# A mixture-of-experts kernel behind strided attention: hints for table jumps in the common part, 32 levels, an earlier load and clears on another engine

## The chip, the core and the metric

The kernel runs on one core of one Trainium2 chip. The time is device microseconds of one execution. A core has TensorE (PE, with its weight loads shown apart as PEld), VectorE (DVE), ScalarE (ACT), GpSimd (POOL) and SyncE (SP, which here issues most transfers), and 16 DMA engines. Each engine has a sequencer of its own that reads its own instructions; a branch is taken by every engine for itself.

## The reference

Two stages in float32. First attention for 8 batches of 8 heads, 576 positions, 64 wide: heads 0 to 3 look back at most 31 positions (local), heads 4 to 7 at every 32nd position (strided). Then each of the 4608 rows (512 wide) goes to the one of eight experts with the highest gate logit; the expert is a two-layer perceptron with 1024 hidden units, and its result is scaled by the gate's probability.

```python
mask_local = (rel >= 0) & (rel < 32)
mask_strided = (rel >= 0) & (pos[None, :] % 32 == pos[:, None] % 32)
...
attn = np.exp(scores - np.max(scores, axis=-1, keepdims=True))
...
for e in range(E):
    h = np.maximum(x_sorted[lo:hi] @ w1[e], 0.0)
    y_sorted[lo:hi] = h @ w2[e]
...
return gate_w[:, None] * y
```

## The kernel before

**Attention.** The program goes through the batches in steps. For a batch SP loads the strided queries and keys (`load_s`: qs and ks, four transfers), the strided values (`load_vs`: vs, four), the local queries and keys (`load_l`: ql and kl, in pieces) and the local values (`load_vl`: vl, four). PE transposes qs and ks (L204) and ql and kl (L192), multiplies queries with keys (L227, L232 and others), and multiplies the weights with vl (L347). Of vl every block of 32 positions is needed twice, for itself and as the block before; POOL makes the second copy (`load_prev`, L123). A few buffers (VL[1], VS[1], BD[0], BD[1]) have parts that must be zero and are never loaded; they are cleared once, by memsets. SP's transfers go in the order in which the program writes them.

**Routing.** The gate's logits give every row its expert and its place in that expert's list. The rows are counted per expert, and the count becomes a level: the number of entries of the table TOTALS that lie under the count (row `lev`, seven DVE instructions from `cnf` to `lvi`). An expert's rows are then rounded up to that entry. By count of this case's data the eight experts have 591, 497, 610, 490, 661, 437, 657 and 665 rows.

**Experts.** For each expert the program has a common part (`first(e)`), which works on the first 256 rows and is the same for any count, and a tail (`rest(e, n)`), which is written out once for every entry n of the table. Between them each engine loads the level (`level`, a TENSOR_LOAD, L869) and takes a jump through a table to the tail of that level (shown as COMPARE_BRANCH, L1196); a tail ends with an unconditional branch to the next common part. `tc.switch_hint` emits, on each engine, an instruction that names the coming jump's target ahead of time (BRANCH_PREFETCH_HINT). In `hid(f, ...)` PE makes one eighth of the hidden layer (L638 to L640: three products, since the float32 numbers are split in a high and a low part), in `mm2c` and `mm2r` the second layer (L916 to L918, L656 to L658). `zs` is a piece of the second layer of the expert before that is left over for the common part and the start of the next tail: `zs((2,))` is step 2 of eight, three matmuls (L656 to L658 of z). `spread` puts pieces of other work between such steps.

Before, a hint for expert 1 stands at the head of `first(1)`, and the hints for experts 2 to 7 in the tail of the expert before, eight steps ahead of its end. The hint for expert 0 and those for the exit of a tail are not part of the change. In the trace COMPARE_BRANCH at L1196 is the jump into a tail as well as the exit out of it.

Of the kernel before, what the change touches and what calls it, by code (L numbers as in the profile page):

```python
# [32 lines left out]
C0 = 256  # L33
N0 = C0 // TM
PB = B - 2
STEPS = range(400, 688, 8)
TOTALS = (C0, 384, *STEPS, 720, CAP)


@with_exitstack  # L40
def kernel(ctx, tc, q, k, v, w_gate, w1, w2, out):
# [42 lines left out]
    def load_s(b):  # L84

        for nm, src, dst in (("qs", q, qs), ("ks", k, ks)):
            t = dst[b] = ld.tile([128, 18 * D], F32, name=nm)
            nc.sync.dma_start(t[:, :16 * D], bass.AP(tensor=src.tensor, offset=base(src, b, 4), ap=[[16 * D, 128], [1, 16 * D]]))
            nc.sync.dma_start(t[:, 16 * D:], bass.AP(tensor=src.tensor, offset=base(src, b, 4) + 64 * 32 * D,
                                                     ap=[[2 * D, 128], [1, 2 * D]]))  # L90

    def load_vs(b):
        for rq in range(4):
            nc.sync.dma_start(VS[b % 2][32 * rq:32 * rq + NB],
                              bass.AP(tensor=v.tensor, offset=base(v, b, 4) + rq * 512,
                                      ap=[[32 * D, NB], [S * D, 4], [1, 512]]))

    def load_l(b, jjs=range(5)):
        for jj in jjs:
            for nm, src, dst in (("ql", q, ql), ("kl", k, kl)):  # L100
                if jj == 0:
                    dst[b] = ld.tile([128, 5, 4, D], F32, name=nm)
                n = 128 if jj < 4 else 64
                nc.sync.dma_start(dst[b][:n, jj], bass.AP(tensor=src.tensor, offset=base(src, b, 0) + jj * 128 * D,
                                                          ap=[[D, n], [S * D, 4], [1, D]]))
# [69 lines left out]
    for i in range(2):  # L175
        V.memset(PST[i][:, :, NB:], 0.0)
    V.memset(VS[0], 0.0)

    wg = const.tile([128, 4, 32], F32)
    V.memset(wg, 0.0)  # L180
# [208 lines left out]
    def lg_a(b):  # L389
        xl, xs = XL.pop(b), XS.pop(b)  # L390
        ls = LS[b] = wk.tile([128, 2, S // 2], F32, name="ls")
        for hf in range(2):
# [15 lines left out]
    colr = const.tile([RT, TM], F32, name="colr")  # L408
    G.iota(colr, pattern=[[1, TM]], base=0, channel_multiplier=0, allow_small_or_imprecise_dtypes=True)
    lev = const.tile([1, len(TOTALS) - 1], F32, name="lev")  # L410
    G.iota(lev[:, 2:2 + len(STEPS)], pattern=[[STEPS.step, len(STEPS)]], base=STEPS.start, channel_multiplier=0,
           allow_small_or_imprecise_dtypes=True)
    for i, n in enumerate(TOTALS[:-1]):
        if n not in STEPS:
# [188 lines left out]
    def gather(e, t, rows=NTOK + 1):  # L603
        G.indirect_dma_start(out=XG[t], out_offset=None, in_=x_out[:rows, :],  # L604
                             in_offset=bass.IndirectOffsetOnAxis(ap=src[:, NT * e + t:NT * e + t + 1], axis=0))
# [91 lines left out]
            return f((n - d) // 5)  # L697

    load_l(0, (2, 3, 4))
    load_vs(0)  # L700
    load_vl(0)
    for n in range(-1, N + 3):
# [8 lines left out]
            open_w()  # L711
        if bb < B:
            if m == 0 and n >= 0:
                if n == 0:
                    load_s(1)
                load_l(bb, (0, 1))
                if n == 0:
                    load_prev(0)
            if m == 1:
                load_l(bb, (2, 3, 4))  # L720
            if m == 2:
                load_vs(bb)
            if m == 3:
                load_vl(bb)
                if bb + 1 < B and n > 0:
                    load_s(bb + 1)
            if m == 4 and n > 0:
                load_prev(bb)
        if n == 0:
            V.memset(VL[1][:, :, 0:1], 0.0)  # L730
            V.memset(BD[0], 0.0)
            blank_s(1)
        if n == 1:
            V.memset(VS[1], 0.0)
            V.memset(BD[1], 0.0)
            blank_l(1)
        if n == 1:
            nc.sync.dma_start(wg[:, :, :8], bass.AP(tensor=w_gate.tensor, offset=w_gate.offset,
# [75 lines left out]
    def settle(n):  # L814
        for _ in range(min(n, len(evs))):
            evs.pop(0)()
# [27 lines left out]
    take(4)  # L844
    rank_c(b)
    slots(slice(N0, NC))
    V.tensor_copy(cnf, cnt)
    V.tensor_tensor(lvc, cnf[:, :, None].to_broadcast([1, E, nl - 1]), lev[:, None, :].to_broadcast([1, E, nl - 1]),
                    op=OP.is_gt)
# [2 lines left out]
    V.tensor_reduce(lvf[:, 2 * E:], lvf[:, E:2 * E], axis=AX.X, op=OP.add)  # L852
    V.tensor_scalar(lvf[:, E:2 * E], lvf[:, E:2 * E], 0.0, float(NTOK), op0=OP.is_gt, op1=OP.mult)
    V.tensor_copy(lvi, lvf)
    for t in range(N0, NT):
        gather(0, t)
    settle(9)
    take(99)
    split2(0, 0)
    settle(9)  # L860
    for i in range(1, 4):
# [124 lines left out]

    def first(e):

        if e == 1:
            tc.switch_hint(lv[e], nl, label=f"e{e}")  # L990
        if e == 0:
            V.memset(YT, 0.0)
            for t in range(NT):
                gather(1, t)
                if t > 2 and t % 2:
                    scatter(0, t // 2 - 1)
        elif e + 1 < E:
            turn()
        if e:
            unturn()  # L1000
        if e == 0:
            for f in refill(0)[1::2]:
                f()
            turn()
        elif e == 1:
            spread(refill(e), [lambda f=f: hid(f, 0, C0) for f in range(6)])
        else:
            zs(range(2, 6))
        if e + 1 < E:
            level(e + 1)  # L1010

    def rest(e, n):
# [7 lines left out]
        nd = direct(w) if last and not one else 0  # L1020
        cy = slice(TM if one else C0 + TM * nd, C0 + w)
        if e > 1:
            zs((6, 7))
            done(e - 1, 0, Z)
            scatter(e - 1, 0)

# [62 lines left out]
        if cy.stop > cy.start:  # L1089
            cols = [mm2c(cy, d) for d in range(4)]  # L1090
            steps += [lambda g=g: next(g) for g in cols for f in range(8)]
        if e and not last:
            steps.insert(max(len(steps) - 8, 0), lambda: tc.switch_hint(lv[e + 1], nl, label=f"e{e + 1}"))
        k = len(todo)
        for i, f in enumerate(steps):
            f()
# [104 lines left out]
```

## Time and profile before

| | |
|---|---|
| time, median of 3 runs | 672.06 us (669.59 to 676.34) |
| time of the profiled execution | 675.38 us |
| span of the profiled execution | 673.5 us |
| mean granted TensorE clock | 0.957 of full speed |
| PE busy | 613.1 us, 91% |
| DVE, ACT, POOL busy | 376.9, 321.6, 202.9 us |

The span goes from the first to the last instruction; the 1.9 us between it and the time lie around it. Busy time is summed per engine, so engines overlap. The granted clock says which share of full speed the throttle gave PE. Attention takes about the first 240 us, the experts the rest.

### The profile page before, as it was taken

The numbers are of one execution on the slowest core, as the hardware profiler recorded it, in microseconds if no ns is written. First come the engines' busy times: TensorE is split into PE (matmuls) and PEld (weight loads), VectorE is DVE, ScalarE is ACT, GpSimd is POOL, SyncE is SP. The second block draws the span as 40 slices with busy tenths as digits, with TensorE's granted clock in tenths as the row PEclk, the third lists the DMA queues.
The fourth block names the chain that finished last, engine by engine and source line by source line (L and its number), as shares of the span: only waits on it lengthen the run. The fifth ranks groups of instructions, "written<-read, shape, count | busy, mean of one in ns | idle before, by whom it ended". The sixth has DMA issues, their size and how long they took to land.

```text
span 673.5 us, 18414 instructions
## 1 busy us (share of the span) xinstructions
PE 613.1 (91%) x7270; PEld 539.7 (80%) x7270; DVE 376.9 (56%) x807; ACT 321.6 (48%) x647; POOL 202.9 (30%) x348
## 2 busy tenths in 40 slices
PE   5589899889996979979999999989999989999995
PEld 4467676667674869979999988879999879999994
DVE  6666888768798663664645346434436534445200
ACT  6457767747765332443543533532534633434311
POOL 0222256236255663503304304303303210110212
PEclk9689999879898889979999999989999989999999
DMA  9897788778635457668899579877368986344101
GB/s 199 172 228 180 188 219 200 178 179 206 162 112 191 153 199 175 165 162 153 294 167 180 212 160 178 295 134 179 141 165 160 260 217 100 148 141 79 51 33 57
DMA packets 237930, 114.02 MB, mean 169 GB/s; under 512 B 209053, under 2 KB 211101, under 8 KB 237728
## 3 DMA queue, kind: packets, MB, share of 16 engines
q1 hardware_dynamic: 230096, 89.70, 55.7%
q0 software_dynamic: 7632, 22.03, 10.9%
q8 instruction: 77, 1.26, 0.8%
q14 instruction: 125, 1.02, 0.5%
HBM read 74.47 MB, written 21.83 MB: 143 GB/s over the span
## 4 chain that ended last, share of the span: by engine, by line
PE 64%; issue 13%; SPq 9%; DVE 4%; ACT 4%; DMA 3%; POOL 2%; POOLq 0%; DVEq 0%; ACTq 0%
PE h L639 7%; PE h L638 7%; PE h L640 7%; SPq L944 5%; PE y L916 4%; PE y L917 4%; PE y L918 4%; PE o L347 2%; PE t L204 2%; PE t L192 2%; PE y L656 2%; PE y L657 2%; PE y L658 2%; SPq L612 2%; PE sc L232 2%
## 5 line engine op out<-in xcount | busy, mean ns | idle before, releaser
L639 PE MATMUL h<-x,w1h 128*128 128x256 f32 (+6 forms) x416 | 133.6, 321 | 3.7 <-issue 3.7
L638 PE MATMUL h<-xh,w1h 128*128 128x256 f32 (+6 forms) x416 | 133.6, 321 | 0.0
L640 PE MATMUL h<-xh,w1l 128*128 128x256 f32 (+6 forms) x416 | 133.3, 320 | 0.0
L645 DVE SCALAR_TENSOR_TENSOR hl<-h,hh 128x256 fp32r<-128x256 f32 (+6 forms) x104 | 52.4, 508 | 125.1 <-ACT hh L644 107.8
L644 ACT ACTIVATE hh<-h 128x256 fp32r<-128x256 f32 (+6 forms) x104 | 46.7, 454 | 117.1 <-PE h L640 104.3
L639 PEld LDWEIGHTS h<-x,w1h 128*128 128x128 f32 x416 | 80.2, 193 | 5.9 <-issue 3.9
L916 PE MATMUL y<-hh,w 128*128 128x408 f32 (+6 forms) x256 | 81.6, 319 | 1.9 <-ACT yt L929 1.4
L638 PEld LDWEIGHTS h<-xh,w1h 128*128 128x128 f32 x416 | 80.1, 193 | 1.9
L917 PE MATMUL y<-hl,w 128*128 128x408 f32 (+6 forms) x256 | 81.3, 318 | 0.2 <-DVE hl L645 0.2
L640 PEld LDWEIGHTS h<-xh,w1l 128*128 128x128 f32 x416 | 80.0, 192 | 1.6
L918 PE MATMUL y<-hh,w 128*128 128x408 f32 (+6 forms) x256 | 81.1, 317 | 0.0
L604 POOL DMA_INDIRECT xg<-xrows,src x48 | 50.9, 1061 | 44.5 <-DMA h<-xg 11.2
L576 DVE TENSOR_TENSOR w1l<-stg,w1h 128x1024 fp32r<-128x1024 f32 x32 | 38.4, 1230 | 39.6 <-ACT w1h L575 36.0
L904 POOL DMA_INDIRECT out_dram<-yo,idx x16 | 15.9, 996 | 140.9 <-ACT yo L662 105.8
L904 POOL DMA_INDIRECT out_dram<-x,idx x32 | 33.7, 1054 | 73.8 <-ACT x L948 34.2
L916 PEld LDWEIGHTS y<-hh,w 128*128 128x128 f32 x256 | 48.0, 188 | 3.0 <-ACT yt L929 2.0
L917 PEld LDWEIGHTS y<-hl,w 128*128 128x128 f32 x256 | 48.1, 188 | 0.7 <-DVE hl L645 0.5
L918 PEld LDWEIGHTS y<-hh,w 128*128 128x128 f32 x256 | 48.1, 188 | 0.0
L582 DVE TENSOR_TENSOR w<-stg,w 128x1024 fp32r<-128x1024 f32 x32 | 39.0, 1223 | 8.6 <-ACT w L581 7.4
L632 DVE TENSOR_TENSOR x<-h,xh 128x512 fp32r<-128x512 f32 x42 | 26.7, 682 | 17.5 <-ACT xh L631 17.5
L581 ACT ACTIVATE w<-stg 128x1024 fp32r<-128x1024 f32 x32 | 33.5, 1053 | 0.0
L575 ACT ACTIVATE w1h<-stg 128x1024 fp32r<-128x1024 f32 x32 | 32.8, 1064 | 0.0
(244 smaller groups left out, 1240.9 us busy)
## 6 DMA issues: line engine op xcount, KB each, us to landing
stg<-in_moe_w_dram SPq DMA_DIRECT2D x64, 512.0 KB
h<-xg SPq DMA_DIRECT2D x112, 96.0 KB
xrows<-xr SPq DMA_DIRECT2D x16, 512.0 KB
x<-yt SPq DMA_DIRECT2D x112, 64.0 KB
qs<-in_q_dram SPq DMA_DIRECT2D x8, 512.0 KB
ks<-in_k_dram SPq DMA_DIRECT2D x8, 512.0 KB
ql<-in_q_dram SPq DMA_DIRECT2D x32, 128.0 KB
kl<-in_k_dram SPq DMA_DIRECT2D x32, 128.0 KB
```

The lines of the kernel that those rows point to most:

```text
L576: V.tensor_tensor(l[:, i], t, h[:, i].bitcast(F32), op=OP.subtract)
L582: V.tensor_tensor(l, t, h.bitcast(F32), op=OP.subtract)
L604: G.indirect_dma_start(out=XG[t], out_offset=None, in_=x_out[:rows, :], in_offset=bass.IndirectOffsetOnAxis(ap=src[:, NT * e + t:NT * e + ...
L638: T.matmul(p, W1H[:, c, fs], x[0][:, c, :n], start=(c == 0), stop=False)
L639: T.matmul(p, W1H[:, c, fs], x[1][:, c, :n], start=False, stop=False)
L640: T.matmul(p, W1L[:, c, fs], x[0][:, c, :n], start=False, stop=(c == 3))
L644: A.activation(h[0][:, f, :n], p, AF.Relu)
L645: V.scalar_tensor_tensor(h[1][:, f, :n], p, 0.0, h[0][:, f, :n].bitcast(F32), op0=OP.max, op1=OP.subtract)
L904: i = G.indirect_dma_start(out=out, out_offset=bass.IndirectOffsetOnAxis(ap=idx[:r, c:c + 1], axis=0), in_=YO[t][:r], in_offset=None, boun ...
L916: T.matmul(p[:, :n], W2H[:, f, ds_], HU[0][:, f, cs], start=(f == 0), stop=False)
L917: T.matmul(p[:, :n], W2H[:, f, ds_], HU[1][:, f, cs], start=False, stop=False)
L918: T.matmul(p[:, :n], W2L[:, f, ds_], HU[0][:, f, cs], start=False, stop=(f == 7))
```

## The change

Five things. The table of levels has 32 steps in place of 40: in place of 384 and every 8 from 400 to 680 it has 384, 416, 448 and every 8 from 480 to 680. SP loads qs and ks of batch 1 ahead of vs and vl of batch 0. Four memsets of zeros move from DVE to POOL, and to an earlier place. The level arithmetic moves behind the remaining gathers of its stage and what they settle. And the hints for experts 1 to 7 move into the common part: for expert 1 after the second of six steps of `hid`, for the others after step 2 of `zs`, while `zs` of steps 3 to 6 stands between the hint and the jump and only step 7 behind it.

```diff
--- before.py
+++ after.py
@@ -33,8 +33,8 @@
 C0 = 256
 N0 = C0 // TM
 PB = B - 2
-STEPS = range(400, 688, 8)
-TOTALS = (C0, 384, *STEPS, 720, CAP)
+STEPS = range(480, 688, 8)
+TOTALS = (C0, 384, 416, 448, *STEPS, 720, CAP)
 
 
 @with_exitstack
@@ -175,6 +175,11 @@
     for i in range(2):
         V.memset(PST[i][:, :, NB:], 0.0)
     V.memset(VS[0], 0.0)
+
+    G.memset(VS[1], 0.0)
+    G.memset(VL[1][:, :, 0:1], 0.0)
+    for i in range(2):
+        G.memset(BD[i], 0.0)
 
     wg = const.tile([128, 4, 32], F32)
     V.memset(wg, 0.0)
@@ -408,7 +413,7 @@
     colr = const.tile([RT, TM], F32, name="colr")
     G.iota(colr, pattern=[[1, TM]], base=0, channel_multiplier=0, allow_small_or_imprecise_dtypes=True)
     lev = const.tile([1, len(TOTALS) - 1], F32, name="lev")
-    G.iota(lev[:, 2:2 + len(STEPS)], pattern=[[STEPS.step, len(STEPS)]], base=STEPS.start, channel_multiplier=0,
+    G.iota(lev[:, 4:4 + len(STEPS)], pattern=[[STEPS.step, len(STEPS)]], base=STEPS.start, channel_multiplier=0,
            allow_small_or_imprecise_dtypes=True)
     for i, n in enumerate(TOTALS[:-1]):
         if n not in STEPS:
@@ -697,6 +702,7 @@
             return f((n - d) // 5)
 
     load_l(0, (2, 3, 4))
+    load_s(1)
     load_vs(0)
     load_vl(0)
     for n in range(-1, N + 3):
@@ -711,8 +717,6 @@
             open_w()
         if bb < B:
             if m == 0 and n >= 0:
-                if n == 0:
-                    load_s(1)
                 load_l(bb, (0, 1))
                 if n == 0:
                     load_prev(0)
@@ -727,12 +731,8 @@
             if m == 4 and n > 0:
                 load_prev(bb)
         if n == 0:
-            V.memset(VL[1][:, :, 0:1], 0.0)
-            V.memset(BD[0], 0.0)
             blank_s(1)
         if n == 1:
-            V.memset(VS[1], 0.0)
-            V.memset(BD[1], 0.0)
             blank_l(1)
         if n == 1:
             nc.sync.dma_start(wg[:, :, :8], bass.AP(tensor=w_gate.tensor, offset=w_gate.offset,
@@ -844,6 +844,10 @@
     take(4)
     rank_c(b)
     slots(slice(N0, NC))
+    for t in range(N0, NT):
+        gather(0, t)
+    settle(9)
+    take(99)
     V.tensor_copy(cnf, cnt)
     V.tensor_tensor(lvc, cnf[:, :, None].to_broadcast([1, E, nl - 1]), lev[:, None, :].to_broadcast([1, E, nl - 1]),
                     op=OP.is_gt)
@@ -852,10 +856,6 @@
     V.tensor_reduce(lvf[:, 2 * E:], lvf[:, E:2 * E], axis=AX.X, op=OP.add)
     V.tensor_scalar(lvf[:, E:2 * E], lvf[:, E:2 * E], 0.0, float(NTOK), op0=OP.is_gt, op1=OP.mult)
     V.tensor_copy(lvi, lvf)
-    for t in range(N0, NT):
-        gather(0, t)
-    settle(9)
-    take(99)
     split2(0, 0)
     settle(9)
     for i in range(1, 4):
@@ -986,8 +986,7 @@
 
     def first(e):
 
-        if e == 1:
-            tc.switch_hint(lv[e], nl, label=f"e{e}")
+        hint = lambda: tc.switch_hint(lv[e], nl, label=f"e{e}")
         if e == 0:
             V.memset(YT, 0.0)
             for t in range(NT):
@@ -1003,9 +1002,12 @@
                 f()
             turn()
         elif e == 1:
-            spread(refill(e), [lambda f=f: hid(f, 0, C0) for f in range(6)])
+            steps = [lambda f=f: hid(f, 0, C0) for f in range(6)]
+            spread(refill(e), steps[:2] + [hint] + steps[2:])
         else:
-            zs(range(2, 6))
+            zs((2,))
+            hint()
+            zs(range(3, 7))
         if e + 1 < E:
             level(e + 1)
 
@@ -1020,7 +1022,7 @@
         nd = direct(w) if last and not one else 0
         cy = slice(TM if one else C0 + TM * nd, C0 + w)
         if e > 1:
-            zs((6, 7))
+            zs((7,))
             done(e - 1, 0, Z)
             scatter(e - 1, 0)
 
@@ -1089,8 +1091,6 @@
         if cy.stop > cy.start:
             cols = [mm2c(cy, d) for d in range(4)]
             steps += [lambda g=g: next(g) for g in cols for f in range(8)]
-        if e and not last:
-            steps.insert(max(len(steps) - 8, 0), lambda: tc.switch_hint(lv[e + 1], nl, label=f"e{e + 1}"))
         k = len(todo)
         for i, f in enumerate(steps):
             f()
```

On SP, around the first batch's loads (vs and vl of batch 0, qs and ks of batch 1; lines are L94 and L113 of `load_vs` and `load_vl`, L88 and L89 of `load_s`), as the difference:

```order
 L104 DMA ql<-in_q_dram 64x4x64
 L104 DMA kl<-in_k_dram 64x4x64
-L94 DMA vs<-in_v_dram 18x4x512 x4
-L113 DMA vl<-in_v_dram 32x18x64 x4
 L88 DMA qs<-in_q_dram 128x1024
 L89 DMA qs<-in_q_dram 128x128
 L88 DMA ks<-in_k_dram 128x1024
 L89 DMA ks<-in_k_dram 128x128
+L94 DMA vs<-in_v_dram 18x4x512 x4
+L113 DMA vl<-in_v_dram 32x18x64 x4
```

The four transfers of qs and ks now stand ahead of the eight of vs and vl.

On POOL, from the constants at the start to the first copies of vl (the names of the cleared buffers are those of the memory that they share), as the difference:

```order
 L140 IOTA cols 128x64
-L409 IOTA colr 96x128
-L411 IOTA lev 1x36
-L417 IOTA prow 96x1
+L179 MEMSET w_63 128x2048
+L180 MEMSET xg 128x2x64
+L182 MEMSET w_62 128x1152
+L182 MEMSET w_63 128x1152
+L414 IOTA colr 96x128
+L416 IOTA lev 1x26
+L422 IOTA prow 96x1
 L123 COPY vl<-vl 32x576
```

Four memsets stand ahead of the last constants and of the first copy.

On PE, in the kernel before, from the end of the last tail written of expert 3 (UNCONDITIONAL_BRANCH) through expert 4's common part to the first rows of the first tail of expert 4 (SWITCH_STRIDE and ISA belong to the jump):

```order
L1196 UNCONDITIONAL_BRANCH
L656 MATMUL z<-w_4604,hh 128x512
L657 MATMUL z<-w_4604,hl 128x512
L658 MATMUL z<-w_4605,hh 128x512
...
L869 TENSOR_LOAD lvi
L1196 SWITCH_STRIDE
L1196 ISA x2
L1118 BRANCH_PREFETCH_HINT
L656 MATMUL z<-w_4604,hh 128x512
L657 MATMUL z<-w_4604,hl 128x512
L658 MATMUL z<-w_4605,hh 128x512
```

Twelve matmuls of z stand ahead of the load of the level and six behind the jump, and there is no hint for the jump here. The same place in the changed kernel:

```order
L1196 UNCONDITIONAL_BRANCH
L661 MATMUL z<-w_4606,hh 128x512
L662 MATMUL z<-w_4606,hl 128x512
L663 MATMUL z<-w_4607,hh 128x512
L989 SWITCH_STRIDE
L989 ISA
L989 BRANCH_PREFETCH_HINT
...
L869 TENSOR_LOAD lvi
L1196 SWITCH_STRIDE
L1196 ISA x2
L1118 BRANCH_PREFETCH_HINT
```

The hint now comes after three matmuls of z; twelve more stand between it and the load of the level, and three behind the jump.

And where the hint was on PE in the kernel before, in the first tail of expert 1:

```order
L638 MATMUL h<-xh,w1h 128x256
L639 MATMUL h<-x_4864,w1h 128x256
L640 MATMUL h<-xh,w1l 128x256
L1093 SWITCH_STRIDE
L1093 ISA
L1093 BRANCH_PREFETCH_HINT
L656 MATMUL y<-w_4604,hh 128x512
L657 MATMUL y<-w_4604,hl 128x512
L658 MATMUL y<-w_4605,hh 128x512
```

It had eight steps of three matmuls of the second layer and two steps of z between it and the branch out of the tail.

## Rows read from the trace of the kernel before

**Rows 1.** The page: engines' busy time, and DMA by queue and kind.

```profile
PE 613.1 (91%) x7270; PEld 539.7 (80%) x7270; DVE 376.9 (56%) x807; ACT 321.6 (48%) x647; POOL 202.9 (30%) x348
...
q8 instruction: 77, 1.26, 0.8%
```

**Rows 2.** Timeline of the start: start, us, engine, line; in brackets idle before, releaser.

```profile
9.45 1.57 SPq L94 DMA_DIRECT2D vs<-in_v_dram  x4
...
15.19 1.48 SPq L88 DMA_DIRECT2D qs<-in_q_dram  x1
...
16.35 0.28 PE L227 MATMUL sc<-mks,identb 128*128 128x144 bf16 x2 [1.69 <-DVE pl L310]
...
17.93 1.21 POOL L123 COPY vl<-vl 32x576 f32<-32x576 f32 x2 [15.49 <-DMA vl<-in_v_dram]
...
22.38 2.56 POOL L123 COPY vl<-vl 32x576 f32<-32x576 f32 x4 [0.19 <-DMA vl<-in_v_dram]
...
24.41 1.08 PE L204 MATMUL t<-ident,qs 128*128 128x128 f32 x4 [7.39 <-DMA qs<-in_q_dram]
...
33.66 0.86 PE L347 MATMUL o<-vl,ptl 64*32 64x64 f32 x64
```

**Rows 3.** Windows of the start: busy us (instructions) by engine, PE clock, DMA share, GB/s.

```profile
17.00:24.40 7.40, 0.02 (x3) 0.02 (x1) 5.01 (x8) 0.00 (x0) 4.45 (x8) 0.59 1.06 219
24.40:34.00 9.60, 9.59 (x213) 7.48 (x213) 5.70 (x14) 7.41 (x17) 0.53 (x1) 0.78 0.61 134
```

**Rows 4.** Groups by shape, 9 to 36 us, DVE: busy, mean ns | idle before.

```profile
L734 DVE MEMSET w<- 128x2048 f32 x1 | 1.8, 1765 | 0.4 <-issue 0.4
L731 DVE MEMSET w<- 128x1152 f32 x1 | 1.0, 1018 | 0.2 <-issue 0.2
```

**Rows 5.** Timeline of PE behind its three longest gaps in the experts' part.

```profile
292.13 0.58 PE L639 MATMUL h<-x,w1h 128*128 128x256 f32 x1 [3.71 <-issue]
...
441.15 0.49 PE L656 MATMUL z<-w,hh 128*128 128x512 f32 x1 [4.33 <-issue]
...
544.28 0.79 PE L656 MATMUL z<-w,hh 128*128 128x512 f32 x1 [2.27 <-issue]
```

**Rows 6.** Windows behind the gaps, and at arrivals in common parts.

```profile
292.20:300.00 7.80, 7.80 (x43) 7.80 (x44) 5.42 (x8) 3.74 (x6) 0.00 (x0) 0.62 0.53 90
442.00:448.00 6.00, 6.00 (x38) 5.61 (x37) 1.19 (x2) 2.41 (x4) 0.98 (x1) 0.75 0.78 142
545.00:550.00 5.00, 5.00 (x30) 4.52 (x29) 0.17 (x1) 1.17 (x3) 0.20 (x1) 0.76 0.59 121
285.40:289.50 4.10, 3.02 (x21) 2.81 (x19) 2.58 (x5) 1.46 (x4) 0.62 (x1) 1.00 1.02 361
333.20:335.60 2.40, 2.40 (x17) 2.14 (x16) 2.40 (x3) 1.10 (x2) 0.00 (x0) 1.00 0.78 243
386.70:387.40 0.70, 0.70 (x6) 0.70 (x5) 0.70 (x2) 0.24 (x1) 0.00 (x0) 1.00 0.04 15
```

**Rows 7.** Line L1196, PE's sequencer, jumps of experts 1, 2, 6: ns, first start.

```profile
L1196 PEldq COMPARE_BRANCH  x1: 302/302/302, 301.6 to 301.6; - x1
...
L1196 PEldq COMPARE_BRANCH  x1: 3193/3193/3193, 334.9 to 334.9; - x1
...
L1196 PEldq COMPARE_BRANCH  x1: 4449/4449/4449, 539.7 to 539.7; - x1
```

**Rows 8.** Lines L1196 and L1118, SP, 322 to 366.5: first and last start.

```profile
L1196 SPq COMPARE_BRANCH  x3: 12/57/81, 322.2 to 365.6; - x3
...
L1118 SPq BRANCH_PREFETCH_HINT  x2: 47/48/50, 327.5 to 366.1; - x2
```

**Rows 9.** Groups by shape, PE: expert 5 (494 to 540 us), z (484 to 500).

```profile
L638 PE MATMUL h<-xh,w1h 128*128 128x440 f32 x32 | 11.6, 363 | 0.0
L916 PE MATMUL y<-hh,w 128*128 128x312 f32 x32 | 9.9, 309 | 1.4 <-ACT yt L929 0.9 <-ACT hh L644 0.5
...
L656 PE MATMUL z<-w,hh 128*128 128x512 f32 x6 | 2.4, 395 | 0.0
```

## The prediction

> **What bounds the kernel now.** I read the page's engine lines first: TensorE (PE) is busy 613.1 of 673.5 us, the next engine 56% [rows 1]. So the time is PE's work, its idle 60 us, and the stretches in which its clock is low. An edit counts only where it alters one of these; a cheaper instruction elsewhere counts where PE waits for it. The second view is PE's own timeline at its long gaps. Four of them touch the change: 7.39 us at the start, up to 24.41 [rows 2], and 3.71, 4.33 and 2.27 us in the expert loop, up to 292.13, 441.15 and 544.28 [rows 5]. The third is the table of windows, for the granted clock behind each gap and for the load on the DMA engines [rows 3, 6].
>
> **The start.** What PE waits for at 24.41 is a DMA, the strided queries of batch 1 (qs) [rows 2]. SP issues them at 15.19, behind four transfers each of vs and vl. In the changed order the qs and ks issues stand where vs stood, 9.45 [rows 2]. That is 15.19 - 9.45 = 5.74 us earlier. With the same flight (24.41 - 15.19 = 9.22 us) qs would be there at 18.67, and of the 7.39 us some 1.65 would stay: 5.7 us gained. What the clock gives on top: PE is granted 0.78 on average from 24.4 to 34.0 while busy 9.59 us [rows 3], and 0.59 in the wait before; busy time at 0.78 costs 9.59 x 0.22 = 2.1 us over full clock. If PE hardly rests, some of that comes back. The upper bound is therefore 7.39 + 2.1 = 9.5.
>
> The lower bound comes from what is now late. The DMA engines are full in the wait, share 1.06 at 219 GB/s [rows 3]; the same bytes must come, in another order. qs and ks of a batch are 2 x 128 x 1152 x 4 B = 1.18 MB, 5.4 us at that rate, and vs and vl now stand behind them. The vl copies on GpSimd (POOL) end at 22.38 + 2.56 = 24.94 [rows 2]; 5.4 us later that is 30.3. PE's first product with vl of this batch (L347) is at 33.66 [rows 2], and would come forward to about 26.3 with the whole wait gone. So PE may wait 4.0 us there: 7.4 - 4.0 = 3.4 us is the lower bound of the gain. Between the ends nothing in the rows decides, since the transfers overlap; I take the middle, **-6.5**, with the clears in it.
>
> The clears: one of 2048 elements a row at 1.77 us, two of 1152 at 1.02 and a small one leave the VectorE (DVE), some 4 us [rows 4]. At 16.35 PE waited 1.69 us for DVE's L310, and the memset of L731 stands 1.02 us in that chain [rows 2, 4]; what remains of the chain is not changed, so I count 0.5 us. On POOL they cost more: no clear of that size runs there in the trace; the nearest row is a copy, 2 x 576 elements a row in 1.21 us, 1.05 ns each [rows 2], so 4480 elements are 4.7 us, against 1765 ns for 2048 on DVE, 0.86 each [rows 4]. POOL sits idle 15.49 us until 17.93 [rows 2], which hides either. If that cover were gone, the copies of vl would be the ones to wait, by the part that sticks out.
>
> **The branch hints.** Each expert's tail is chosen by a table jump (L1196) in a common part. Before, the hint for expert e + 1 stands in the tail of expert e, eight steps before its end; now it stands in the common part, three matmuls after arrival. Two things can stall PE there: a new block of code that the sequencer must have, and the jump itself. The page's row of instruction fetches is 77 packets and 1.26 MB on PE's queue, 16.4 KB each [rows 1]; by count of the built kernels such a block holds 256 PE instructions. The gap at 292.13 comes four matmuls after arrival in expert 1's common part, that at 441.15 after twelve in expert 4's; counted in the built kernel before, the two places lie 64,512 = 252 x 256 instructions apart, so both stand at the end of a block. The gap at 544.28 is no block's end: there the jump took 4.45 us [rows 7].
>
> Prices of the jump, by the row of each: 0.30 us (expert 1), 3.19 (2), 4.45 (6) [rows 7]. The jump's own time doesn't show on PE where matmuls are queued: expert 2's 3.19 us leave no gap, since twelve matmuls stand ahead, at 0.395 us each up to 4.7 us of work, part of it already done [rows 7, 9]. The cheap jumps and crossings are where DMA is quiet, the dear ones where it is full: share 1.02 at expert 1's arrival, 285.4, and 0.78 at expert 2's, 333.2, against 0.04 at expert 3's, 386.7, where no gap follows [rows 6].
>
> What is removed: idle 3.71 + 4.33 + 2.27 = 10.3 us [rows 5], and the slow clock behind the gaps. The granted clock is 0.62 for 7.8 us behind the first, 0.75 for 6 us behind the second, 0.76 for 5 us behind the third [rows 6]: 7.8 x 0.38 = 3.0, 6 x 0.25 = 1.5 and 5 x 0.24 = 1.2, together 5.7 us. The old places cost **16.0**.
>
> What is added: moving the hints and dropping eight table entries shifts every block's end. Counted in the changed kernel, experts 1 and 4 no longer cross one behind few matmuls, but expert 2's common part does, right after the three matmuls of its first step; its arrival, with a DMA share of 0.78, is nearer to that of the 3.71 us than to the quiet one [rows 5, 6], so 3 to 4.5 us idle, and some 1.2 of clock: 4.7 with 3.5 of it. Expert 5's part crosses behind fifteen matmuls and in quiet DMA: 0.5. For the jumps of experts 4 and 6 fifteen matmuls stand ahead now where twelve did, 3 x 0.395 = 1.2 us more cover [rows 9]; expert 6 keeps 2.27 - 1.2 = 1.1 and 1 of clock, expert 4, whose jump stood behind its crossing before, about 1.7 by the same reckoning. Expert 1, hint after two of six steps: 0.5. Sum 4.7 + 0.5 + 2.1 + 1.7 + 0.5 = 9.5, with 1 for what I can't see: 10.5. Net **-5.5**. The bounds are far apart: -13 with expert 2's crossing covered and the hints working, +6 with two places more of the 4.33 kind.
>
> Do hints in the same block help at all? SP shows both kinds: expert 1's jump at 322.2, hinted in its own common part, is followed by the tail's first instruction at 327.5; expert 2's at 365.6, hinted in the tail before, by that at 366.1 [rows 8]. That is 5.3 us against 0.5, speaks against the new place, and is why I count the hint itself as worth nothing, only the shift of the places and the longer cover. On SP 5 us more per expert are hidden: the three gaps of rows 5 are all of over 2 us that PE has in the experts' part, and none lies near 327.5 [rows 5].
>
> [...]
>
> **The smaller parts.** The levels: only expert 5's changes, 440 to 448 columns. At 440 a matmul is 363 ns and at 312 309 ns [rows 9]; (363 - 309) / 128 = 0.42 ns a column, x 8 columns x 192 matmuls = **+0.65**. The level arithmetic (seven DVE instructions) goes behind gathers that PE doesn't wait for: 0, or 0.2 either way.
>
> **Sum.** -6.5 - 5.5 + 0.65 = -11.35 us, from the profiled run's 675.38 to 664.0. That run is 0.5% above the median of the three, 672.06; scaled, the forecast is **661**.
>
> **The rivals.** (a) The new hints do nothing and each place costs what it did, only elsewhere: net 0 for them, -6.5 + 0.65, 666. For it: the SP rows. Against: the two block ends do move. (b) Crossings are hidden and the hints hold: -11.5 to -17 for them, 650 to 656. For it: jumps of 0.30 us exist [rows 7]; against: the arrivals of experts 1, 4 and 6 stalled [rows 5]. (c) The start gives nothing: the same bytes at full share, and L347 waits for vl instead of L204 for qs; -0.5 - 5.5 + 0.65, 667, to 673 where the hints give little too. Against: the vl copies are 8.7 us ahead of L347 now, 24.94 against 33.66 [rows 2]. (d) Slower: every one of the six common parts of experts 2 to 7 stalls as expert 4's did, 4.33 and 1.5 of clock [rows 5, 6], because a hint three matmuls after arrival starts a fetch that throws out the block being run or the next one. That is 6 x 5.83 = 35 against 16.0 removed, +19 - 6.5 + 0.65: 685. It equals the time before from 3.6 us a part on, and is over 1% slower from 4.8.
>
> **How the numbers follow.** Chances: forecast 0.55, (a) 0.2, (b) 0.1, (c) 0.1, (d) 0.05. The runs before spread over 669.6 to 676.3, so 1% (665.3, 678.8) is about what can be told from no change. The forecast's own cases lie in 655 to 667, nearly all faster; with (b), and a little of (a) and (c), faster is 0.67, same 0.28, slower 0.05. The range takes in the whole of the forecast and (a), the near end of (b) and all of (c): 650 to 674.
>
> **What would show it.** PE's wait for qs at L204 should be under 3 us, with qs issued near 9.5; a new wait at L347 for vl would be the loss. No gap of over 3 us before expert 1's L639 line or in expert 4's common part; one of 3 to 4.5 us in expert 2's. Jumps at L1196 still of 3 to 4 us in full DMA, hidden behind fifteen matmuls. DVE free of L730 to L735, POOL with some 5 us of memset before its first copy. Wrong would be: gaps at all of the common parts (d), or none (b), or qs landing no earlier (c).

## The result and the profile after

The changed kernel takes 680.69 us (median of 21 runs, 673.75 to 688.51), the kernel before 671.36 (21 runs, 666.48 to 679.73). The ratio is 1.0122, interval 1.0093 to 1.0151: about 8 us slower, where 11 us faster were forecast. Times here are medians of all runs, while a ratio compares only those runs of both kernels that lie within 1.5% of their kernel's fastest, so the two can differ by a few us. The profiled execution after took 680.05 us with a span of 678.0; that of before, 675.38, is 4 us above its kernel's median, and so the two spans show less than the whole difference.

The engine totals of the page after hardly differ from [rows 1]: PE is as busy, so the loss is waits.

```profile
PE 613.7 (91%) x7270; PEld 537.1 (79%) x7270; DVE 376.7 (56%) x805; ACT 321.7 (47%) x647; POOL 207.5 (31%) x352
...
q8 instruction: 76, 1.25, 0.9%
```

**The start** went as the steps said, at its own place. The timeline of the start after (start, us, engine, line; in brackets idle before and releaser; L209 and L352 are L204 and L347 of before):

```profile
10.26 0.60 SPq L88 DMA_DIRECT2D qs<-in_q_dram  x1
...
12.40 1.53 SPq L94 DMA_DIRECT2D vs<-in_v_dram  x4
...
17.36 0.28 PE L232 MATMUL sc<-mks,identb 128*128 128x144 bf16 x2 [1.21 <-DVE pl L315]
17.96 0.66 PE L209 MATMUL t<-ident,qs 128*128 128x128 f32 x4
...
23.80 5.05 POOL L123 COPY vl<-vl 32x576 f32<-32x576 f32 x8 [17.41 <-DMA vl<-in_v_dram]
...
29.59 0.86 PE L352 MATMUL o<-vl,ptl 64*32 64x64 f32 x64
```

The wait of 7.39 us for qs [rows 2] is gone; L209 starts at 17.96 in place of 24.41. The copies of vl end at 23.80 + 5.05 = 28.85, 3.9 us later than before, but PE comes to them at 29.59 without a wait of note. The wait at L232 is 1.21 in place of 1.69 us: 0.5 for the clears, as forecast.

**The jumps** did not. The gaps of PE in the experts' part after, from its timeline; the rows of before are [rows 5]:

```profile
332.60 0.49 PE L661 MATMUL z<-w,hh 128*128 128x512 f32 x1 [1.83 <-issue]
...
390.06 0.49 PE L661 MATMUL z<-w,hh 128*128 128x512 f32 x1 [1.68 <-issue]
...
439.48 0.79 PE L661 MATMUL z<-w,hh 128*128 128x512 f32 x1 [3.13 <-issue]
...
500.83 0.50 PE L661 MATMUL z<-w,hh 128*128 128x512 f32 x1 [1.95 <-issue]
...
548.26 0.66 PE L661 MATMUL z<-w,hh 128*128 128x512 f32 x1 [3.80 <-issue]
...
608.84 0.49 PE L661 MATMUL z<-w,hh 128*128 128x512 f32 x1 [1.04 <-issue]
```

Six gaps, one behind the jump of each of experts 2 to 7: 13.4 us. Before there were two at such a place, 6.6 us. The jumps themselves, from line L1196 on PE's sequencer (ns, first start), experts 2 to 7 in turn:

```profile
L1196 PEldq COMPARE_BRANCH  x1: 5260/5260/5260, 327.2 to 327.2; - x1
L1196 PEldq COMPARE_BRANCH  x1: 5177/5177/5177, 384.7 to 384.7; - x1
L1196 PEldq COMPARE_BRANCH  x1: 5426/5426/5426, 433.9 to 433.9; - x1
L1196 PEldq COMPARE_BRANCH  x1: 4637/4637/4637, 496.0 to 496.0; - x1
L1196 PEldq COMPARE_BRANCH  x1: 6050/6050/6050, 542.1 to 542.1; - x1
L1196 PEldq COMPARE_BRANCH  x1: 4885/4885/4885, 603.8 to 603.8; - x1
```

All take 4.6 to 6.1 us. Before, the same six took 3.19, 1.14, 3.59, 0.62, 4.45 and 1.47 [rows 7 show the first and the fifth]. The trace also has the packets by which PE's sequencer gets its code, 16.4 KB each (1.25 MB in 76 by the page after; between 20 and 240 us of the kernel before 37 of them come for 4645 matmuls and 4646 weight loads, one for 251 of both). The packets' times and sizes are on record, but not which code they bring; that is inferred from their place. Between arrival in expert 3's common part and the first instruction of its tail there are two of them after, and one before. DMA by queue in that stretch, after (381.69 to 389.97), then before (386.71 to 390.15): queue and kind, packets, MB, share:

```profile
q8 instruction: 2, 0.03, 1.7%
```

```profile
q8 instruction: 1, 0.02, 2.2%
```

By the packets' times the first starts 0.74 us behind the arrival in both kernels. In the kernel before it lasts 1.21 us, and the tail's first instruction comes 1.5 us behind its end. In the changed kernel a second one follows, 2.7 us behind the start of the jump, 0.97 us long, and the tail begins 1.56 us behind that. From arrival to tail it is 8.28 us in place of 3.44; 4.0 us of the difference is the longer jump, with the second packet in it, and 0.8 us that the jump comes later.

The execution as a whole has no more packets than before, 76 against 77 by the pages. In the kernel before, one packet starts 1.2 to 2.7 us behind each of the six hints, still ahead of the exit out of the tail; in the changed kernel the last 10 us ahead of each exit hold none. So the second packet looks like the fetch of the jump's target, moved from the tail into the wait.

### The profile page after: what moved, and what is told of

It reads as the page before. It is cut to its first block, busy times and chain, and to the rows that moved or that the text cites. A ratio compares the mean times of both kernels' runs of the same rounds, so it can differ in the third digit from the quotient of the medians.

```text
span 678.0 us, 18423 instructions
## 1 busy us (share of the span) xinstructions
PE 613.7 (91%) x7270; PEld 537.1 (79%) x7270; DVE 376.7 (56%) x805; ACT 321.7 (47%) x647; POOL 207.5 (31%) x352
## 3 DMA queue, kind: packets, MB, share of 16 engines
q8 instruction: 76, 1.25, 0.9%
q14 instruction: 148, 1.21, 0.7%
## 4 chain that ended last, share of the span: by engine, by line
PE 47%; issue 15%; SPq 13%; DMA 7%; ACT 7%; DVE 7%; POOL 3%; POOLq 0%; DVEq 0%; ACTq 0%
SPq L944 7%; PE h L643 5%; PE h L644 5%; PE h L645 5%; SPq L617 5%; DMA stg<-in_moe_w_dram 3%; PE y L916 2%; PE y L917 2%; PE y L918 2%; PE sc L304 2%; PE o L352 2%; PE t L209 2%; PE o L281 2%; PE t L197 2%; PE t L334 2%
## 5 line engine op out<-in xcount | busy, mean ns | idle before, releaser
L916 PE MATMUL y<-hh,w 128*128 128x408 f32 (+6 forms) x256 | 82.7, 323 | 5.4 <-ACT yt L929 3.4
L918 PE MATMUL y<-hh,w 128*128 128x408 f32 (+6 forms) x256 | 81.9, 320 | 0.0
L609 POOL DMA_INDIRECT xg<-xrows,src x48 | 51.3, 1068 | 49.1 <-DMA x<-yt 16.4
L916 PEld LDWEIGHTS y<-hh,w 128*128 128x128 f32 x256 | 48.8, 191 | 6.8 <-ACT yt L929 4.2
L918 PEld LDWEIGHTS y<-hh,w 128*128 128x128 f32 x256 | 48.9, 191 | 0.0
L661 PE MATMUL z<-w,hh 128*128 128x512 f32 x56 | 23.4, 418 | 13.5 <-issue 13.4
```

The costliest lines, as they stand in the source:

```text
L916: T.matmul(p[:, :n], W2H[:, f, ds_], HU[0][:, f, cs], start=(f == 0), stop=False)
L918: T.matmul(p[:, :n], W2L[:, f, ds_], HU[0][:, f, cs], start=False, stop=(f == 7))
```

## The experiments

A block is here what one packet brings, the exit is the branch out of a tail, and the arrival is the end of the exit. The theory that the trace suggests (theory 1): every arrival in a new part starts a fetch of the next block by itself; a jump waits for what is being fetched; and a target that was not fetched ahead costs one fetch more behind the arrival. The expert part below is the span less the start of expert 0's jump at L1196, one profiled execution each; by it before has 673.5 - 255.3 = 418.2 us and the changed kernel 678.0 - 245.9 = 432.1. "Arrival to tail" is summed over the jumps of experts 2 to 7, from the end of the exit to the first instruction of the tail, on PE's sequencer. As each row is one execution, a difference of a few us in the expert part is not certain; the sums of the arrivals differ far more.

| kernel | ratio to before (interval) | expert part, us | arrival to tail, us | PE idle there, us |
|---|---|---|---|---|
| before | 1 | 418.2 | 28.4 | 6.6 |
| changed | 1.0122 (1.0093 to 1.0151) | 432.1 | 47.1 | 13.4 |
| x1 tail hints | 0.9926 (0.9886 to 0.9965) | 418.1 | 26.8 | 4.1 |
| x2 no hints | 1.0091 (1.0052 to 1.0130) | 428.1 | 48.1 | 14.4 |
| x3 before, common hints | 1.0115 (1.0067 to 1.0163) | 430.6 | 48.1 | 13.4 |
| x4 before, early load | 0.9881 (0.9832 to 0.9930) | 414.4 | 26.5 | 4.8 |
| x5 tail hints, more cover | 0.9839 (0.9787 to 0.9891) | 411.9 | 31.4 | 0.7 |
| x6 common hints, more cover | 1.0111 (1.0061 to 1.0161) | 431.7 | 55.9 | 13.9 |
| x7 late tail hints | 0.9910 (0.9873 to 0.9947) | 413.7 | 24.5 | 1.7 |

**x1: the hints, and with them the split of zs, back as they were; all else as changed.**

```diff
-        hint = lambda: tc.switch_hint(lv[e], nl, label=f"e{e}")
+        if e == 1:
+            tc.switch_hint(lv[e], nl, label=f"e{e}")
...
-            zs((2,))
-            hint()
-            zs(range(3, 7))
+            zs(range(2, 6))
...
+        if e and not last:
+            steps.insert(max(len(steps) - 8, 0), lambda: tc.switch_hint(lv[e + 1], nl, label=f"e{e + 1}"))
```

> The changed kernel with the hints for experts 1 to 7 (and the split of zs) back where they stood before; the early load, the clears, the 32 levels and the moved level arithmetic stay. Theory 1, fetches in series: on arrival in a common part PE's sequencer fetches the next block of code by itself, and a hint behind the arrival only queues the target's fetch after that, so the jump waits for two fetches; with the hint ahead of the exit it waits for one. Then the jumps at L1196 of experts 2 to 7 fall from 4.6 to 6.1 us back to 0.6 to 4.5, and the time to 660 to 666 us, ratio 0.98 to 0.99, since the start keeps its 9 us. Rival, phases: the jumps are dear because the whole expert part starts 9 us earlier against the transfers; then they stay near 5 us and the time stays at 675 to 682, ratio 1.005 to 1.015.

The jumps fall back, and with them the time: 667.6 us, ratio 0.9926 against 1.0122. The hints' place, with the split of zs that goes with it, is therefore worth 1.0122 / 0.9926 = 1.97%, 13 us (10 to 16 by the two intervals), on the same start and the same levels. The rival, phases, is out: x2 and x5 below both reach expert 0's jump at 250.6 us, and only x2 has the dear jumps. Experts 3, 4 and 5 on PE's sequencer, line L1196:

```profile
L1196 PEldq COMPARE_BRANCH  x1: 1418/1418/1418, 385.7 to 385.7; - x1
L1196 PEldq COMPARE_BRANCH  x1: 5183/5183/5183, 430.9 to 430.9; - x1
L1196 PEldq COMPARE_BRANCH  x1: 1083/1083/1083, 492.1 to 492.1; - x1
```

The instruction packets between arrival and tail are one for each of the six again. What stays, as at expert 4, is that one fetch coming late: 3.62 us behind the arrival, against 0.73 and 0.74 at experts 3 and 5. The ratio is a little worse than the range expected.

**x2: no hints for experts 2 to 7.**

```diff
             zs((2,))
-            hint()
             zs(range(3, 7))
```

> The changed kernel without any hint for the jumps of experts 2 to 7 (expert 1's stays). Theory 1: a hint that close to its jump is worth nothing, so jumps without one cost the same 4.6 to 6.1 us, time within 3 us of the changed kernel's, ratio to before 1.007 to 1.017. Rival, the hint does harm (it starts a fetch that throws out a block in use): without it each part is 1.5 to 3 us shorter, time 665 to 672, ratio 0.99 to 1.00.

679.82 us, ratio 1.0091: the changed kernel's within the intervals. Line L1195 (one line less than above), experts 3 and 5:

```profile
L1195 PEldq COMPARE_BRANCH  x1: 5198/5198/5198, 389.2 to 389.2; - x1
...
L1195 PEldq COMPARE_BRANCH  x1: 4958/4958/4958, 497.0 to 497.0; - x1
```

With a hint they were 5177 and 4637 ns; over the six jumps it is 4.4 to 7.1 us without a hint and 4.6 to 6.1 with it. On PE the hint in the common part is void for these experts: no help or harm shows in the time, and the harm that rival (d) of the prediction gave it is out.

**x3: the kernel before with the new hints alone.**

```diff
-        if e == 1:
-            tc.switch_hint(lv[e], nl, label=f"e{e}")
+        hint = lambda: tc.switch_hint(lv[e], nl, label=f"e{e}")
...
-            zs(range(2, 6))
+            zs((2,))
+            hint()
+            zs(range(3, 7))
```

> The kernel before with one part of the change alone: hints for experts 1 to 7 in the common part, with the changed split of zs; 40 levels, start as before. Theory 1: two fetches at each of six jumps, 4.6 to 6 us each; expert 1's gap of 3.7 us goes or stays with the block end; time 680 to 688, ratio 1.013 to 1.025. Rival, phases: the jumps stay at 0.6 to 4.5 us and the time within 1% of before.

682.64 us, ratio 1.0115: inside the time that theory 1 gave, a little under its ratio. The jumps take 3.9 to 5.7 us, with two packets behind each of the six arrivals. The loss comes with the hints and their split of zs alone. Expert 1's gap stays here (3.23 us). x3 and the changed kernel differ only by the start, the clears, the levels and the level arithmetic, and their ratios are 1.0115 and 1.0122: beside the dear jumps these four together gave nothing that shows (0.0007, with some 0.0056 of uncertainty).

**x4: the kernel before with the early load alone.**

```diff
     load_l(0, (2, 3, 4))
+    load_s(1)
     load_vs(0)
...
-                if n == 0:
-                    load_s(1)
```

> The kernel before with the early load of qs and ks of batch 1 alone; the clears stay on VectorE, hints and levels as before. Theory 1: the start gives 7 to 9.5 us and all of it stays, 662 to 664, ratio 0.986 to 0.99, jumps as before (0.6 to 4.5 us). Rival, phases or given back: PE reaches expert 0 some 8 us earlier, but meets later rows and weights or dearer jumps, so that half or more is lost again: 667 to 671, ratio 0.994 to 1.0.

668.35 us, ratio 0.9881: some 8 us, which looks like the whole start. By the medians of all runs (671.93 before, in the same series) it is 3.6 us, so the size is not sharp. The traces speak against the whole start, too. PE's first L204 (L209) of a batch is a landmark that all kernels share. The rows for batch 1 are above and in [rows 2]. Here are batch 3 and batch 7 from PE's timeline, in the kernel before:

```profile
71.37 0.66 PE L204 MATMUL t<-ident,qs 128*128 128x128 f32 x4
...
171.64 0.90 PE L204 MATMUL t<-ident,qs 128*128 128x128 f32 x4
```

in x4:

```profile
69.61 0.66 PE L204 MATMUL t<-ident,qs 128*128 128x128 f32 x4
...
167.07 0.66 PE L204 MATMUL t<-ident,qs 128*128 128x128 f32 x4
```

and in x3, which has the old start:

```profile
69.02 0.66 PE L204 MATMUL t<-ident,qs 128*128 128x128 f32 x4
...
165.87 0.66 PE L204 MATMUL t<-ident,qs 128*128 128x128 f32 x4
```

Over the seven kernels with the early load (changed, x1, x2, x4 to x7) and the three without (before, x3, x8), the mean start of batch 1 is 17.8 against 24.2, of batch 2 42.9 against 46.0, of batch 3 69.1 against 70.9, of batch 5 117.3 against 117.6; the first load of a level comes at 241.5 against 242.6. So 6.4 us are gained at batch 1 and mostly given back in the four batches behind it; by these means about 1 us reaches the experts. That figure is rough: the single executions lie between 238.1 and 243.1 with the early load, and between 239.9 and 246.0 without. Against the profiled execution of before, x4 has 3.8 us of its gain in the expert part: 418.2 to 414.4. There expert 1's crossing of a block's end (a gap of 3.71 us; one of 1.53 us at another place stays) and expert 4's second fetch are gone (its arrival to tail falls from 8.04 to 4.84 us, two packets to one). By count of the built kernels PE's program ahead of the experts is three instructions longer in x4, so I take this for the ends of blocks and not for the load; no run shows it by itself.

Some of the expert part's gain is lost again to another wait: the tail of expert 5 in x4, from PE's and ScalarE's timelines:

```profile
520.80 0.63 PE L915 MATMUL y<-hh,w 128*128 128x312 f32 x1 [3.83 <-ACT yt L928]
```

```profile
520.37 0.28 ACT L926 ACTIVATE yt<-y 128x128 f32<-128x128 f32 x1 [6.09 <-DMA stg<-in_moe_w_dram]
```

PE waits 3.83 us for ScalarE, which had stood 6.09 us before that, until weights came. In the seven kernels with the early load PE idles 5.1 to 8.3 us in such tails, in before and x3 1.9 and 3.2. Why the early load goes with it is not settled.

**x5: tail hints, and all of zs but its last step between arrival and jump.**

```diff
-            zs(range(4 if last else 2))
+            zs(range(4 if last else 0))
...
-            zs((2,))
-            hint()
-            zs(range(3, 7))
+            zs(range(7))
...
+        if e and not last:
+            steps.insert(max(len(steps) - 8, 0), lambda: tc.switch_hint(lv[e + 1], nl, label=f"e{e + 1}"))
```

> The changed kernel with the hints for experts 2 to 7 back in the tails, and more work between arrival and jump: steps 0 to 6 of zs, 21 matmuls at 0.4 us, all stand in the common part (before: steps 0 and 1 in the tail, 2 to 5 in the common part). Theory 1: one fetch after arrival, resume 3.1 to 6.1 us after arrival as in x1; 8 us of queued work hide all of them, so the gaps of 1.7 to 2.4 us at experts 4 and 6 go: 4 us and their slow clock, ratio 0.98 to 0.988. Rival, the cover doesn't matter because PE's queue holds only a few matmuls ahead of its sequencer: gaps stay within 1 us of x1's, ratio 0.99 to 0.995.

664.85 us, ratio 0.9839, the lowest of the kernels here. The jumps of experts 4 and 6 still take over 3 us, and PE doesn't stand: its only gap at the six jumps is 0.67 us at expert 5, where the jump takes 4.2 us. Line L1196, experts 4, 5 and 6:

```profile
L1196 PEldq COMPARE_BRANCH  x1: 3103/3103/3103, 426.6 to 426.6; - x1
...
L1196 PEldq COMPARE_BRANCH  x1: 4172/4172/4172, 484.3 to 484.3; - x1
...
L1196 PEldq COMPARE_BRANCH  x1: 3307/3307/3307, 532.2 to 532.2; - x1
```

Twenty-one queued matmuls hide a jump with one fetch behind the arrival, and all but 0.67 us of expert 5's, where a second packet starts 1.7 us behind the start of the jump although the hint stands in the tail. Why this one comes is open.

**x6: the same cover, with the hint first in the common part.**

```diff
-            zs(range(4 if last else 2))
+            zs(range(4 if last else 0))
...
-            zs((2,))
-            hint()
-            zs(range(3, 7))
+            hint()
+            zs(range(7))
```

> The changed kernel with the hint as the first thing in the common part of experts 2 to 7 and steps 0 to 6 of zs (21 matmuls, 8 us) between it and the jump. Theory 1: two fetches still start one after the other behind each arrival, the second at 4 to 6 us; the jump now comes some 4 us later than in the changed kernel, so it takes 1 to 3 us in place of 4.6 to 6.1, and the gaps (1.0 to 3.8 us) mostly go: 8 to 12 us better than the changed kernel, ratio 0.995 to 1.004. Rival, a hint in the block of its jump is void whatever stands between: the jump stays at 4.5 us and more, ratio 1.008 to 1.015.

The theory fell here, as far as the hint goes, and the rival held: 682.61 us, ratio 1.0111. The hint is now 1.9 to 5.4 us ahead of its jump (0.8 to 3.3 in the changed kernel), and the jumps take what they took, L1195, experts 2, 3 and 5:

```profile
L1195 PEldq COMPARE_BRANCH  x1: 5823/5823/5823, 328.8 to 328.8; - x1
L1195 PEldq COMPARE_BRANCH  x1: 4584/4584/4584, 386.9 to 386.9; - x1
L1195 PEldq COMPARE_BRANCH  x1: 5180/5180/5180, 496.6 to 496.6; - x1
```

The second packet starts 0.9 to 3.5 us behind the start of the jump (mean 2.5; in the changed kernel 1.9 to 3.0, mean 2.6; in x2, with no hint, 1.9 to 4.7, mean 2.7), though the jump comes 0.3 to 4.6 us later behind the arrival than in the changed kernel. So the hint doesn't start it; by its place, the jump does. More cover also buys nothing, as the jump moves behind the added matmuls, and its 5 us begin later: PE idles 13.9 us at the six arrivals, 13.4 in the changed kernel.

**x7: tail hints behind the last step, only zs of steps 0 and 1 and the exit behind them.**

```diff
-        if e and not last:
-            steps.insert(max(len(steps) - 8, 0), lambda: tc.switch_hint(lv[e + 1], nl, label=f"e{e + 1}"))
...
+        if e and not last:
+            tc.switch_hint(lv[e + 1], nl, label=f"e{e + 1}")
         if e:
             zs(range(4 if last else 2))
```

(against x1.)

> The changed kernel with the hints for experts 2 to 7 in the tails, but behind their last step, with only two steps of zs (six matmuls) and the exit behind them, in place of eight steps ahead of the end. Theory 1 in the form that lead counts: the hint's fetch starts 1 to 2.7 us behind it, about at the exit, and the arrival's own fetch follows it: two fetches again or one and a half, resume 5 to 7 us after arrival, ratio 0.995 to 1.005. In the form that the side of the exit alone counts: one fetch after arrival, jumps as in x1, ratio 0.99 to 0.996.

667.52 us, ratio 0.9910, x1's. With 2.4 to 4.1 us of lead, inside the 1.9 to 5.4 that x6 had, there is one packet behind every arrival, and the jump of expert 3 takes 854 ns, that of expert 4 3494 (L1196):

```profile
L1196 PEldq COMPARE_BRANCH  x1: 854/854/854, 382.0 to 382.0; - x1
...
L1196 PEldq COMPARE_BRANCH  x1: 3494/3494/3494, 427.4 to 427.4; - x1
```

Lead doesn't decide between x6 and x7; the side of the exit does. And the hint need not have brought its block before the exit: between hint and exit there is no packet at all here, and the page counts 70 where x1 has 76, one less for each of the six jumps:

```profile
q8 instruction: 70, 1.15, 0.8%
```

The one packet behind the arrival is enough. Whether it is then the jump's target or the block that theory 1 lets every arrival fetch, the trace doesn't say; for theory 1 as it stands it is one packet too few.

**x8: useless transfers in the quiet arrivals (kernel before).** SP issues four copies of 512 KB between places of device memory at the end of the tails of experts 2, 4 and 6; the output is not touched.

```diff
+        if e in (2, 4, 6):
+            for i in range(4):
+                j = 4 * (e // 2 - 1) + i
+                nc.sync.dma_start(junk[128 * j:128 * j + 128], w1[0, 128 * i:128 * i + 128, :])
         if e:
             zs(range(4 if last else 2))
```

> The kernel before with 2 MB of useless transfers (four of 512 KB, from one place of device memory to another) that SP issues at the end of the tails of experts 2, 4 and 6, so that the arrivals in the common parts of experts 3, 5 and 7, quiet until now, meet busy DMA engines. If the fetch's delay comes from the load on the DMA engines, the arrival's fetch starts 2 to 3 us after arrival there in place of 0.73 to 0.79, and these jumps take 2.5 to 4.5 us in place of 0.6 to 1.5; experts 2, 4, 6 stay as they are. If it comes from something else (which tail is left, the block's place), nothing changes at experts 3, 5 and 7.

Inconclusive: SP came to them at 384.15, 2.1 us behind PE's arrival in expert 3's common part (382.02), and the fetch had started at 1.21 us in a quiet stretch. Windows of x8 at the arrival and behind it (the last three columns are PE clock, DMA share, GB/s):

```profile
382.00:383.20 1.20, 1.20 (x9) 1.20 (x8) 1.20 (x2) 0.26 (x1) 0.00 (x0) 1.00 0.02 9
...
386.00:392.00 6.00, 6.00 (x28) 4.93 (x27) 0.08 (x1) 0.00 (x0) 0.00 (x0) 1.00 1.05 400
```

It is one run of 684.86 us; what it shows is that the added transfers cost elsewhere: PE idles 4.7 us in expert 3's tail and 8.4 in expert 5's, behind ScalarE, which waits for a transfer (in expert 5's tail for weights).

No run has the same transfers set earlier, the changed kernel without expert 1's hint or with that hint later, or the kernel before with the 32 levels alone.

## Why the prediction was wrong

**The hints** (-5.5 forecast, bounds -13 and +6) are the step that failed: by x1 they cost 13 us, by x3 alone 1.15%, 8 us (interval 4.5 to 11; why the two differ is open). The step was "I count the hint itself as worth nothing, only the shift of the places and the longer cover". It took the jump's prices from rows that all belong to jumps with a hint (0.30 to 4.45 us; those of experts 2 and 6 with a hint ahead of the exit), and asked what a useless new hint adds. But a useless new hint comes with the loss of a useful old one, and the price of that is an unhinted jump: 4.4 to 7.1 us in x2. The trace of before held a branch without a hint, that of the `tc.If` at the very end of the kernel, and it was not weighed. The row, line L1130 of before, PE's sequencer:

```profile
L1130 PEldq COMPARE_BRANCH  x1: 4826/4826/4826, 662.5 to 662.5; - x1
```

Twelve packets stand in the six arrivals in place of seven, and the arrivals are 47.1 - 28.4 = 18.7 us longer on the sequencer. Queued matmuls hide more than half of that: PE idles 13.4 us there against 6.6.

**SP's row was read rightly**: the 5.3 us against 0.5, which it says "speaks against the new place" [rows 8], are what the change does on SP too. From the jump of expert 2 to the tail's first instruction SP takes 0.43 us before and 3.79 in the changed kernel, 3.94 in x2. It should have gone into the sum for PE, where the same two places for a hint exist.

**The places.** Expert 1's gap of 3.71 us went, as forecast (1.12 us for another reason stays), and so did expert 4's stall ahead of its jump. The 3.5 us of a crossing in expert 2's part didn't show: its gap of 1.83 us stands behind the jump. My count of block ends by the program fits the two places of before, and was not reliable for the changed kernel.

**The start** (-6.5) was right at its place, 6.4 us at batch 1, no wait at L352, so the lower bound's rival wait didn't come. It was mis-sized for the total: by the landmarks about 1 us reaches the experts, though single executions scatter by more. The times agree that part is lost: x1, which has the start, the clears, the levels and the level arithmetic, gains 0.74%, 5 us (2.4 to 7.7), and between x3 and the changed kernel the same four give nothing that shows. How much the start alone is worth stays open. The forecast took a wait that falls early in a pipeline of eight batches as time off the end, though the rows show DVE busy for 21.33 and PE for 22.52 of 24.00 us in a batch of the steady part, 72 to 96 us (windows of the kernel before):

```profile
72.00:96.00 24.00, 22.52 (x629) 16.86 (x628) 21.33 (x61) 17.27 (x39) 11.60 (x26) 1.00 0.86 217
```

Which of PE's work, VectorE's or the transfers (share 0.86) takes the lead back is not shown.

**The clears** cost POOL 1.81 + 0.21 + 2.07 = 4.1 us (4.7 by the copy), early and hidden. **The levels**: 128x448 takes 365 ns where 128x440 took 363, and 128x320 315 for 309 [rows 9], so (2 + 6) x 96 ns = 0.8 us for 0.65, by these means. **The level arithmetic**, 0.2 us either way by the forecast, fits: PE's gap ahead of its first matmul of the second layer is 2.40 us before and 2.59 in the changed kernel, 2.40 to 2.41 and 2.59 to 2.60 in the others without and with the arithmetic moved (and 32 levels).

Of the rivals, (d) had the sign and the place, six common parts, at 685 for 680.7, with 5% and the wrong cause: it let the hint throw out a block, and x2 shows that the hint does nothing (jumps of 4.4 to 7.1 us without it, 4.6 to 6.1 with it). It charged 5.83 us a part, where the gaps are 1.0 to 3.8, so that its total came near by luck. (a), "The new hints do nothing", had the cause, and a price of nought for it.

**Left open.** Expert 1's hint, in its own common part, goes with a jump of 0.31 us in all the kernels here, with 7.3 to 15.7 us of lead. Whether that hint works since the lead is longer, or expert 1's target is at hand for another reason, no run shows. On SP a long lead didn't help: in the kernel before, SP's hint for expert 1 stands in the same part, at 290.2, 32 us ahead of the jump at 322.2, and the tail still starts at 327.5 [rows 8], 5.2 us behind the jump; in the changed kernel, with 2.6 us of lead, it is 5.3. That the arrival's own fetch starts late because the transfers fill the DMA engines is what the rows suggest (0.7 to 0.8 us behind the arrival at experts 3, 5 and 7 of nearly all kernels, 1.8 to 4.3 at most of the others; DMA share 0.04 against 0.78 and 1.02 [rows 6]), but x8 didn't force it.

## What to carry to other kernels

For the jumps of experts 2 to 7 a hint was of use ahead of the branch that leads into the jump's own part; there 2.4 to 4.1 us of lead were enough (x7, ratio 0.9910). Behind that branch it did nothing for these six of PE's jumps, at any lead up to 5.4 us (x6, 1.0111; x2, with no hint, 1.0091). When an edit moves a hint, price the jump without any hint from a row of an unhinted jump in the same trace (here 4.83 us at L1130 of before), and add that for each jump. A wait that is removed at the start of a pipeline counts only as far as a landmark at its end moves: compare the start of the same operation in later batches before taking it off the time (here 6.4 us at batch 1, about 1 us at the first load of a level). And where an edit moves code, a gap may go with it: expert 1's 3.71 us of before are gone in x4, whose program ahead of the experts is three instructions longer. That such a gap is the end of a block is an estimate from the counted places; no run shows it by itself.

## What was not expected of the hardware

A packet follows the arrival even when the jump's target was hinted: at least one of 16.4 KB behind each of the six arrivals in the kernel before, the changed one, x1, x3 and x7, 0.9 to 1.3 us long in the kernel before, and mostly some 1.5 us from the last one's end to the tail's first instruction. A jump right behind an arrival seems to wait for it: with the hint in the tail no tail starts earlier than 3.1 us behind its arrival. In x7 this packet is all there is between the hint and the tail. Cover by queued matmuls, as in x5, hides that (PE idles 0.7 us at the six arrivals); an earlier hint doesn't: x7 with 2.4 to 4.1 us of lead and x1 with 6.0 to 8.8 sum to 24.5 and 26.8 us from arrival to tail.
